# Another written order for the same operations of attention and a two-layer network

## The chip, the cores and the metric

The kernel runs on one core of a Trainium2 chip. A core has five engines, each with its own list of instructions: PE (TensorE, matrix multiplication), ACT (ScalarE), DVE (VectorE), POOL (GpSimd) and SP (SyncE, which here only issues transfers). DMA transfers are issued by SP, ACT or POOL. The metric is the time of one execution on the device in microseconds (us); lower is better. The numbers of runs are medians.

## The reference

Eight batches of eight heads have 576 tokens of 64 dimensions each, and every head has 16 extra "beacon" keys and values that stand ahead of its own and that every token sees. Causal attention over them gives 4608 rows of 512 features; these go through a layer of 2048 units with a squared ReLU and back to 512.

```python
k_all = np.concatenate([beacon_k, k], axis=2)
v_all = np.concatenate([beacon_v, v], axis=2)
scores = scale * np.matmul(q, k_all.transpose(0, 1, 3, 2))
scores = np.where(causal, -1000000000.0, scores)
...
a = np.exp(scores)
a /= a.sum(-1, keepdims=True) + 1e-09
attn = np.matmul(a, v_all)
...
h = x @ w_in
r = np.maximum(h, 0.0)
g = r * r
return (g @ w_out).astype(np.float32)
```

Inputs and the output are fp32; the kernel multiplies in bf16.

## The kernel before

The work is cut into 1553 operations. Each has a name, an engine or a choice of engines, the operations that it needs, and the buffers that it takes from small pools: two pairs of PSUM banks for scores (`strip`), four single banks (`ps`), six fp32 staging buffers (`stg`). The string `SEQUENCE` at the head of the file (lines 16 to 149) writes the names in one order. `Order.run` walks it word by word, takes the buffers, and emits the operation's instructions; a letter behind `@` says on which engine (A is ACT, D is DVE, P is POOL). Nothing is rearranged afterwards, so this one string sets the order on each engine, the order in each queue of transfers, and which buffer each operation gets. An engine takes its instructions strictly in that order: one that waits holds up all behind it.

The names that matter below:

- `fldq`, `fldk`: the first loads of batch 0's q (issued by ACT into osb1) and k (issued by SP into osb0), for the first 240 tokens: head pair 0 alone, pair 1 alone, and pairs 2 and 3 together. `fcq`, `fck` cast them to bf16 (L351 is a copy or cast on ACT, L353 one on DVE or POOL).
- `sld`: loads that cast on the way (L473), issued by POOL, for the rest of batch 0's q and k and all of batch 1's. `two` joins two heads of such a load side by side. `ld` (L397, L398) loads 128 tokens into a staging buffer, and `cast` turns them to bf16: so come the v of batches 0 and 1 (POOL's queue) and everything of the later batches (SP's queue). `bkl` loads the beacon keys (L443).
- `ident`, `tri`: the identity matrix and the causal mask, made by POOL. `fill`: sixteen dummy matrix multiplications of 128x512 that only keep PE busy (L485).
- `tp`: transposes on PE of q and k of batches 0 and 1 (L511), copied out of PSUM by ACT or DVE (`eq`, `ek`); `tpb` does the beacon keys (L453). Later batches are transposed by DMAs on SP's queue (`tr`, L432).
- `qk`: scores (L649); `exp`: their exponentials on ACT (L671 in batch 0, L747 later); `mask` (L770, DVE); `av`: weighted sums of v (L792); `norm`: division by the sums (L809, L811, DVE). `xtp`, `xte` (L860) and, from batch 3 on, transposing DMAs `xt` (L843) bring the result to xT.
- `s1`: the first layer of a chunk of 512 tokens (L1094, in the last two chunks L971), then `relu` and `sq` on ACT or DVE; `s2`: the second layer (L1144, L1203), its evacuations `ev` (L351, L353, L1226), and the stores `st` (L1132; in the last chunk L1257). From the third chunk on the second layer, and in the last two also the first, replaces one of eight block products by sums (`wsum`, `asum`, `xsum`, `sum`). `win` and `wout` (L884, L892) load the weights in quarters by POOL's queue. The first load of batch 2 waits for the quarter `wout3`.

Batches 0 and 1 go through PE transposes and start the pipeline; then the scores of a batch, the first layer of a chunk and the second layer of the chunk before are woven into one stream on PE.

Of the kernel before, what the change touches and what calls it, by code (L numbers as in the profile page):

```python
# [16 lines left out]
fldk1 fldk0 bkl0 fldk2 sld0q1.0 sld0k1.0 ident sld0k1.2 sld0q1.2 tri ld0v0 ld0v1 ld0v2 ld0v4 fldq0 fldq2 fldq1 fcq2@A  # L17
bkc0 fck2 fill14 fill1 fill3 fill0 fill4 fill9 fill7 tp0.0.2q tp0.0.2k tpb0 fcq1 tp0.0.1q fck3 fcq3@D fcq0 ek0.0.2@D
ekb0 fck1 bkl1 ld0v3 two0.1.3k@P sld1q0.0 sld1k0.0 two0.1.3q@P cast0v0@P win0 cast0v2 cast0v4 sld1k0.2 cast0v3 ld1v4
win1 sld1q0.2 two1.0.0k@P win3 ld1v2 ld1v3 two1.0.2k@P cast1v4 win2 ld1v1 ld1v0 wout0 wout1 two1.0.2q@P wout3 wout2  # L20
two1.0.3k@P cast1v3 cast1v1 cast1v2 cast1v0 two1.0.3q@P fck0 tpg0.0.2k eq0.0.2@A tpg0.0.2q tp0.0.1k tp0.0.3k ek0.0.1@A
ek0.0.3@A tpg0.0.3k tpg0.0.1k qk2.0.0 tp0.0.0q exp2.0.0 eq0.0.0@A two0.1.1q@D eq0.0.1@D tp0.0.3q fill10 two0.1.0q@D
eq0.0.3@D tpg0.0.1q tpg0.0.0q two0.1.0k@D two0.1.1k@D tpg0.0.3q qk1.0.0 exp1.0.0 qk3.0.0 fill13 tp0.0.0k tp0.1.1k
ek0.0.0@A tpg0.0.0k bkc1 ek0.1.1@D tpg0.1.1k exp3.0.0 fill15 tp0.1.1q qk0.0.0 fill5 tp0.1.0q fill6 eq0.1.1@A tpg0.1.1q
eq0.1.0@D mask2.0.0 exp0.0.0 qk1.1.0 tp0.1.0k qk1.1.1 exp1.1.0 ek0.1.0@D mask3.0.0 two0.1.2q@D mask0.0.0 two0.1.2k@D
tpg0.1.0q qk0.1.0 exp1.1.1 exp0.1.0 mask1.1.1 mask1.0.0 cast0v1@D fill11 qk1.1.2 fill2 tp0.1.2k tp0.1.3k tp0.1.3q
qk0.1.1 exp1.1.2 ek0.1.2@A mask1.1.0 eq0.1.3@A ek0.1.3@D tpg0.1.2k tpg0.1.3k tpg0.1.3q tpg0.1.0k mask0.1.1 qk0.1.2
exp0.1.1 exp0.1.2 av1.0.0 fill8 av3.0.0 qk3.1.0 tp0.1.2q norm1.0.0 norm3.0.0 eq0.1.2@A mask0.1.0 tpg0.1.2q av0.0.0
av2.0.0 norm0.0.0 two1.0.0q@D exp3.1.0 norm2.0.0 qk3.1.1 xtp0.0.3 av1.1.0 xte0.0.3@A exp3.1.1 norm1.1.0 fill12 qk2.1.0
exp2.1.0 two1.0.1k@D two1.0.1q@D mask2.1.1 mask3.1.1 qk3.1.2 tpb1 xtp0.0.0 mask3.1.0 ekb1 av0.1.0 xte0.0.0@A norm0.1.0  # L30
qk2.1.2 tp1.0.0k tp1.0.0q tp1.0.1q exp3.1.2 exp2.1.2 ek1.0.0 tpg1.0.0k qk2.1.1 eq1.0.0@D eq1.0.1@A tpg1.0.1q tpg1.0.0q
exp2.1.1 av3.1.0 xtp0.0.2 xtp0.0.1 xte0.0.1@A norm3.1.0 tp1.0.1k xte0.0.2@A qk4.2 xtp0.1.3 mask2.1.0 ek1.0.1 tpg1.0.1k
xte0.1.3@D exp4.2.1.0.0 exp4.2.0.0.0 av2.1.0 s1.0.1.0 s1.0.2.0 norm2.1.0 xtp0.1.0 xtp0.1.1 qk4.4 relu0.1.0@A mask4.0.0
xte0.1.0@A xte0.1.1@D relu0.2.0@A exp4.4.0.0.0 s1.0.4.0 xtp0.1.2 s1.0.5.0 xte0.1.2@D relu0.5.0@A s1.0.0.0 s1.0.1.1
tp1.0.2k relu0.0.0@D relu0.4.0@D exp4.4.1.0.0 relu0.1.1@A s1.0.0.1 ek1.0.2 relu0.0.1@A s1.0.7.0 s1.0.3.0 relu0.7.0@A
relu0.3.0@D s1.0.5.1 relu0.5.1@A tp1.0.2q eq1.0.2@A s1.0.3.1 s1.0.6.0 tpg1.0.2q tpg1.0.2k qk5.7 relu0.3.1@D
relu0.6.0@A sq0.2.0@A exp5.7.-1.0.0 s1.0.4.1 relu0.4.1@A exp5.7.-1.1.0 sq0.1.0@A s1.0.6.1 s1.0.15.1 relu0.6.1@D
mask4.0.2 sq0.0.1@D s1.0.13.0 s1.0.12.1 relu0.15.1@A mask4.0.1 relu0.13.0@A relu0.12.1@A exp5.7.1.0.0 sq0.3.0@A
s1.0.7.1 s1.0.13.1 s1.0.14.1 relu0.7.1@D relu0.13.1@A s1.0.9.1 relu0.9.1@A s1.0.9.0 s1.0.8.1 relu0.14.1@A relu0.9.0@D
sq0.0.0@A relu0.8.1@D s1.0.11.1 s1.0.11.0 s1.0.10.1 relu0.11.0@D sq0.2.1@A relu0.11.1@D av4.0.0 s1.0.2.1 av4.0.1  # L40
sq0.3.1@A relu0.10.1@D exp5.7.0.0.0 relu0.2.1@A norm4.0.0 sq0.5.1@D norm4.0.1 s1.0.14.0 relu0.14.0@A s1.0.8.0
relu0.8.0@A sq0.1.1@A sq0.7.1@D sq0.4.1@A s1.0.10.0 s1.0.15.0 s1.0.12.0 relu0.12.0@A sq0.6.0@A relu0.10.0@D sq0.5.0@A
s2.0.2.0 relu0.15.0@D tp1.0.3k sq0.6.1@A mask5.0.1 s2.0.2.1 tp1.0.3q s2.0.0.0 ek1.0.3 sq0.7.0@D mask5.0.0 tpg1.0.3k
eq1.0.3@A tpg1.0.3q qk7.13 exp7.13.-1.1.0 exp7.13.-1.0.0 sq0.4.0@D exp7.13.0.0.0 exp7.13.1.0.0 s2.0.0.1 wsum1
mask5.0.2 av5.0.0 s2.0.3.0 norm5.0.0 s2.0.0.2 s2.0.2.2 s2.0.0.3 s2.0.3.1 ev0.0@A qk6.10 exp6.10.-1.1.0 exp6.10.-1.0.0
zero2 ld2k0 ld2q0 ld2q1 ld2q2 ld2q3 ld2k1 cast2q1 cast2q0 cast2k0 cast2q3 cast2q2 ld2q4 ld2k2 cast2q4 cast2k1 ld2k3
ld2k4 cast2k2 cast2k3 tr2q cast2k4 tr2k ld2v0 ld2v1 ld2v2 ld2v3 ld2v4 ld3k0 zero3 cast2v2 cast2v0 s2.0.3.2 av5.0.1
s2.0.2.3 s2.0.3.3 s2.0.1.0 mask7.0.1 wsum2 exp6.10.1.0.0 exp6.10.1.0.1 exp6.10.0.0.0 ev0.2@A mask6.0.0 mask6.0.2
mask7.0.2 mask7.0.0 mask6.0.1 norm5.0.1 ev0.3@A av6.0.0 av7.0.0 av6.0.1 s2.0.1.1 norm7.0.0 norm6.0.0 av7.0.1 xtp1.0.1
norm6.0.1 xte1.0.1@D norm7.0.1 s2.0.1.2 xtp1.0.2 xtp1.0.0 xtp1.0.3 s2.0.1.3 xte1.0.3@D xte1.0.2@A xte1.0.0@A ev0.1@A  # L50
warm s1.1.14.0 s1.1.13.0 relu1.13.0@D s1.1.6.0 s1.1.1.0 s1.1.9.0 relu1.14.0@A relu1.6.0@D s1.1.12.0 s1.1.4.0
relu1.1.0@A relu1.9.0@A relu1.12.0@D st0 cast2v4 cast2v3 cast2v1 ld3q0 cast3q0 ld3q1 ld3q2 cast3q1 ld3q3 ld3k1 ld3q4
ld3k2 cast3q3 cast3q2 cast3k1 ld3k3 ld3k4 cast3q4 st1 tr3q cast3k0 cast3k3 cast3k2 cast3k4 tr3k ld3v0 ld3v1 ld3v2
cast3v2 cast3v0 ld3v3 cast3v3 cast3v1 ld3v4 ld4k0 ld4q0 ld4q1 ld4q2 cast4k0 cast3v4 qk8.4 exp8.4.1.0.0 exp8.4.0.0.0
s1.1.0.0 s1.1.3.0 s1.1.15.0 relu1.0.0@D relu1.15.0@D sq1.0.0@D relu1.4.0@A qk8.2 exp8.2.0.0.0 s1.1.7.0 s1.1.2.0
s1.1.5.0 relu1.7.0@A exp8.2.1.0.0 relu1.2.0@D relu1.3.0@A sq1.1.0@A mask8.0.1 relu1.5.0@D mask8.0.2 sq1.2.0@D
# [1304 lines left out]
```

## Time and profile before

| | |
|---|---|
| median of 3 runs | 330.6 us (330.38 to 331.23) |
| profiled execution, its span from the first instruction to the last | 329.0 us |
| median less that span | 1.6 us |
| PE busy in the span | 314.3 us (96%) |
| DVE, ACT, POOL busy | 235.9, 218.2, 100.5 us |
| granted TensorE clock, mean | 1.000 |

For the profiled execution the profile gives its span; the row below that is the difference to the runs' median. In the views, PEld is the weight load of TensorE, which runs beside PE, and SPq, ACTq and POOLq are the engines' queues in the act of issuing a transfer. "<-" behind a row names what the engine waited for.

### The profile page before, as it was taken

The numbers are of one execution on the slowest core, as the hardware profiler recorded it, in microseconds if no ns is written. First come the engines' busy times: TensorE is split into PE (matmuls) and PEld (weight loads), VectorE is DVE, ScalarE is ACT, GpSimd is POOL, SyncE is SP. The second block draws the span as 40 slices with busy tenths as digits, with TensorE's granted clock in tenths as the row PEclk, the third lists the DMA queues.
The fourth block names the chain that finished last, engine by engine and source line by source line (L and its number), as shares of the span: only waits on it lengthen the run. The fifth ranks groups of instructions, "written<-read, shape, count | busy, mean of one in ns | idle before, by whom it ended". The sixth has DMA issues, their size and how long they took to land.

```text
span 329.0 us, 8399 instructions
## 1 busy us (share of the span) xinstructions
PE 314.3 (96%) x3407; PEld 225.1 (68%) x3428; DVE 235.9 (72%) x503; ACT 218.2 (66%) x324; POOL 100.5 (31%) x157
## 2 busy tenths in 40 slices
PE   4789999999999999999999999999999999999995
PEld 1357885554556448778886566666878788888884
DVE  1799467445745699758973878657788699598982
ACT  2599996546953996678577567679852493895710
POOL 8997704414504704025032502531200320000000
PEclk9999999999999999999999999999999999999999
DMA  8999998999999995299999997998941500011033
GB/s 165 215 213 224 220 187 193 200 196 241 234 199 194 235 210 108 65 185 216 182 191 195 214 202 192 215 171 172 180 111 66 136 2 0 2 61 68 3 143 114
DMA packets 145601, 51.97 MB, mean 158 GB/s; under 512 B 132506, under 2 KB 140570, under 8 KB 145562
## 3 DMA queue, kind: packets, MB, share of 16 engines
q1 hardware_dynamic: 135901, 42.32, 62.7%
q0 software_dynamic: 8512, 8.49, 15.1%
q10 hardware_dynamic: 1149, 0.62, 0.7%
q8 instruction: 27, 0.44, 0.6%
q14 instruction: 12, 0.10, 0.1%
HBM read 37.22 MB, written 9.44 MB: 142 GB/s over the span
## 4 chain that ended last, share of the span: by engine, by line
PE 76%; DMA 9%; SPq 6%; DVE 3%; POOL 2%; issue 2%; ACT 1%; POOLq 0%; DVEq 0%; ACTq 0%
PE ps L1094 24%; PE ps L1203 18%; PE ps L1144 8%; PE ps L792 8%; PE strip L649 4%; PE strip L971 4%; DMA stg<-in_v_dram 3%; PE ps L971 3%; PE strip L1203 2%; DMA osb<-in_k_dram 2%; SPq L843 2%; SPq L432 2%; PE ps L649 1%; SPq L398 1%; DMA stg<-in_q_dram 1%
## 5 line engine op out<-in xcount | busy, mean ns | idle before, releaser
L1094 PE MATMUL ps<-xT,w_in 128*128 128x512 bf16 (+6 forms) x627 | 103.7, 314 | 1.0 <-DMA xT<-xn 0.3
L747 ACT ACTIVATE pt<-strip 128x1024 bf16<-128x1024 f32 (+3 forms) x77 | 71.0, 958 | 15.4 <-PE strip L649 14.3
L1094 PEld LDWEIGHTS <-w_in 128*128 128x128 bf16 x640 | 56.9, 98 | 35.4 <-issue 1.9
L1109 ACT ACTIVATE g<-ps 128x512 bf16<-128x512 f32 (+2 forms) x74 | 38.9, 545 | 27.1 <-PE ps L1094 26.0
L353 POOL CAST qk_area<-stg 128x512 bf16<-128x512 f32 (+2 forms) x60 | 39.6, 685 | 54.6 <-DMA stg<-in_q_dram 49.5
L353 POOL CAST vb<-stg 128x512 bf16<-128x512 f32 (+1 forms) x39 | 25.8, 682 | 82.7 <-DMA stg<-in_v_dram 69.3
L1111 DVE TENSOR_SCALAR g<-ps 128x512 bf16<-128x512 f32 (+2 forms) x54 | 33.2, 623 | 23.5 <-PE ps L1094 23.0
L1203 PEld LDWEIGHTS <-g 128*128 128x128 bf16 x448 | 42.5, 98 | 7.3 <-issue 1.8
L770 DVE TENSOR_TENSOR pt<-pt,tri 128x512 bf16<-128x512 bf16 (+1 forms) x93 | 37.6, 427 | 6.7 <-ACT pt L747 6.4
L792 PEld LDWEIGHTS <-pt 128*128 128x128 bf16 x930 | 35.5, 99 | 7.1 <-issue 0.9
L792 PE MATMUL ps<-vb,pt 128*128 128x65 bf16 x930 | 38.1, 194 | 0.8 <-POOL vb L353 0.6
L1203 PE MATMUL ps<-w_out,g 128*128 128x256 bf16 x304 | 38.8, 273 | 0.0
L1203 PEld LDWEIGHTS <-sum_area 128*128 128x128 bf16 x336 | 31.8, 98 | 5.5 <-issue 1.0
L811 DVE TENSOR_TENSOR xn<-ps,rcp 128x320 bf16<-128x320 f32 (+2 forms) x64 | 31.5, 491 | 2.5 <-DVE rcp L809 0.4
L1119 ACT ACTIVATE g<-g 128x1024 bf16<-128x1024 bf16 (+2 forms) x35 | 31.5, 928 | 0.5
L1144 PE MATMUL ps<-w_out,g 128*128 128x512 bf16 x120 | 29.9, 379 | 0.4
L747 ACT ACTIVATE pt<-ps 128x512 bf16<-128x512 f32 x42 | 23.6, 600 | 8.5 <-PE ps L649 8.5
L649 PE MATMUL strip<-qT,kT 64*128 64x208 bf16 (+15 forms) x406 | 27.4, 255 | 0.7 <-ACT pt L671 0.4
L649 PEld LDWEIGHTS <-kT 64*128 64x128 bf16 x520 | 17.3, 94 | 15.0 <-issue 10.3
L1203 PE MATMUL ps<-w_sum,sum_area 128*128 128x256 bf16 x208 | 26.7, 273 | 0.0
L809 DVE RECIPROCAL rcp<-ps 128x5 f32<-128x5 f32 (+2 forms) x64 | 12.1, 189 | 16.2 <-PE ps L792 15.2
L351 ACT COPY osb<-ps 128x512 f32<-128x512 f32 x22 | 12.9, 588 | 15.5 <-PE ps L1203 11.6
(99 smaller groups left out, 375.1 us busy)
## 6 DMA issues: line engine op xcount, KB each, us to landing
out_dram<-osb SPq DMA_DIRECT2D x16, 512.0 KB, 4.1
stg<-in_q_dram SPq DMA_DIRECT2D x24, 256.0 KB, 4.8
stg<-in_k_dram SPq DMA_DIRECT2D x18, 256.0 KB, 4.4
stg<-in_v_dram SPq DMA_DIRECT2D x18, 256.0 KB, 4.6
w_in<-in_moe_w_in_dram POOLq DMA_DIRECT2D x4, 512.0 KB, 9.1
w_out<-in_moe_w_out_dram POOLq DMA_DIRECT2D x4, 512.0 KB, 12.3
stg<-in_v_dram POOLq DMA_DIRECT2D x6, 256.0 KB, 8.5
stg<-in_k_dram SPq DMA_DIRECT2D x6, 224.0 KB, 4.2
```

The lines of the kernel that those rows point to most:

```text
L353: eng[e].tensor_copy(dst, src)
L649: nc.tensor.matmul(out, kT[b % 2][hp, pr, 128 * c:128 * c + 128], rhs, start=True, stop=True)
L747: nc.scalar.activation(out, in_, AF.Exp, bias=0.0, scale=scale)
L770: nc.vector.tensor_tensor(out=d, in0=d, in1=tri[0:rows, m0:m0 + m, 0:w][:, None].to_broadcast([rows, 2, m, w]), op=ALU.min)
L792: nc.tensor.matmul(a[0:w, at + (t - tl[0]) * (D + 1):at + (t - tl[0] + 1) * (D + 1)], P[0:rr, hj, o:o + w], vb[b % 2][0:rr, c, 2 * pr + hj ...
L811: nc.vector.tensor_tensor(out=xn[b % 2].rearrange("p t (h d) -> p h t d", d=D)[:, h0:h0 + nh, tl[0]:tl[0] + nt], in0=a[:, :, :, 0:D], in1= ...
L1094: nc.tensor.matmul(h[:, lo - spans[0][0]:hi - spans[0][0]], w_in_sb[:, mc, ft * 128:(ft + 1) * 128], xT[:, mc, lo % RING:lo % RING + hi - lo],
L1109: nc.scalar.activation(dst, h, AF.Relu, bias=0.0, scale=1.0)
L1111: nc.vector.tensor_scalar(out=dst, in0=h, scalar1=0.0, scalar2=None, op0=ALU.max)
L1119: nc.scalar.activation(d, d, AF.Square, bias=0.0, scale=1.0)
L1144: nc.tensor.matmul(o, G[:, fc, ts * 128:(ts + 1) * 128], w_out_sb[:, fc, :], start=(fc == 0), stop=(fc == NFT - 1))
L1203: nc.tensor.matmul(o, lhs[:, f, t * 128:(t + 1) * 128], rhs[:, f], start=fresh and f == 0, stop=f == HF - 1, skip_group_check=True)
```

## The change

Only the string `SEQUENCE` differs. It holds the same 1553 names in another order, with other letters for 152 of them: 77 go from DVE to ACT, 69 from ACT to DVE, three from POOL to DVE and three from DVE to POOL. The new string is a line longer, so that every line of the code behind it has a number higher by one. The head and the end of the difference:

```diff
 SEQUENCE = """
-fldk1 fldk0 bkl0 fldk2 sld0q1.0 sld0k1.0 ident sld0k1.2 sld0q1.2 tri ld0v0 ld0v1 ld0v2 ld0v4 fldq0 fldq2 fldq1 fcq2@A
...
-ev8.c22.1 s2.8.3.1 s2.8.4.1 ev8.c12.0 ev8.c21.0@D st8.0.1.0 st8.0.0.256 st8.0.0.0 st8.1.0.0 ev8.c12.1 ev8.c21.1@A
-st8.0.1.256 st8.1.1.0
...
+ev8.c21.0@D st8.1.0.0 s2.8.3.0 ev8.c12.0 st8.0.0.256 ev8.u2.1@A s2.8.7.1 ev8.u3.1@A s2.8.5.1 s2.8.4.1 ev8.c21.1@A
+ev8.c22.1 s2.8.3.1 st8.0.0.0 ev8.c12.1 st8.0.1.256 st8.1.1.0
```

On ACT at the start of the program, before (osb1 is where q of batch 0 is loaded, qT and kT hold the transposed q and k, strip the scores; a load of 120x2x128 is one head pair, one of 120x4x128 is two):

```order
L554 DMA osb1_83<-in_q_dram 120x2x128
L554 DMA osb1_83<-in_q_dram 120x4x128
L554 DMA osb1_83<-in_q_dram 120x2x128
L351 ACT_TABLE_LOAD
L351 CAST qk_area_64<-osb1_83 120x2x2x64 x3
L351 COPY qT0_68<-ps3_94 128x240
L351 COPY kT0_70<-ps1_92 128x240
L351 COPY kT0_70<-ps0_91 128x240
L671 ACTIVATE pt_72<-strip0_89 128x2x368
```

The same place after:

```order
L555 DMA osb1_83<-in_q_dram 120x4x128
L555 DMA osb1_83<-in_q_dram 120x2x128 x2
L352 ACT_TABLE_LOAD
L352 CAST qk_area_64<-osb1_83 120x2x2x64 x2
L352 COPY qT0_68<-ps2_93 128x240
L352 CAST qk_area_64<-osb1_83 120x2x2x64
L352 COPY kT0_70<-ps0_91 128x240
L352 COPY qT0_68<-ps3_94 128x240
L352 COPY qT0_68<-ps1_92 128x240
L672 ACTIVATE pt_72<-strip0_89 128x2x368
```

The load of two pairs of q is now the first; the two single ones follow, pair 1 and then pair 0. The cast of q's pair 2 has gone to DVE, and that of pair 3 has come from there. On SP's queue, in the same way, the load of k for pairs 2 and 3 moved from the fourth place to the second, and pair 0's from the second to the fourth.

On POOL at the start, before (stg are the staging buffers of v, qk_area takes the casting loads of q and k):

```order
L473 DMA qk_area_64<-in_q_dram 112x4x192
L473 DMA qk_area_64<-in_k_dram 112x4x192
masks.py:197 MEMSET ident_77 128x128
masks.py:199 ISA
masks.py:199 AFFINE_SELECT ident_77<-ident_77 128x128
L473 DMA qk_area_64<-in_k_dram 112x4x192
L473 DMA qk_area_64<-in_q_dram 112x4x192
L336 MEMSET tri_88 128x512
L338 AFFINE_SELECT tri_88<-tri_88 128x128 x4
L397 DMA stg_63<-in_beacon_v_dram 16x8x64
L398 DMA stg_63<-in_v_dram 112x8x64
L398 DMA stg_63<-in_v_dram 128x8x64 x2
```

The same place after:

```order
L399 DMA stg_63<-in_v_dram 128x8x64
masks.py:197 MEMSET ident_77 128x128
masks.py:199 ISA
masks.py:199 AFFINE_SELECT ident_77<-ident_77 128x128
L474 DMA qk_area_64<-in_q_dram 112x4x192
L474 DMA qk_area_64<-in_k_dram 112x4x192
L337 MEMSET tri_88 128x512
L339 AFFINE_SELECT tri_88<-tri_88 128x128 x4
L474 DMA qk_area_64<-in_q_dram 112x4x192
L474 DMA qk_area_64<-in_k_dram 112x4x192
L474 DMA qk_area_64<-in_q_dram 96x4x384
L398 DMA stg_63<-in_beacon_v_dram 16x8x64
```

One load of v (`ld0v3`) goes ahead of the identity, all four casting loads behind it, and the first casting load of batch 1 (96x4x384) ahead of the other four loads of v.

On ACT at the end of the program, before (g holds the squared first layer of the last chunk, osb the output on its way to the store):

```order
L1048 ACTIVATE g_80<-g_80 128x1024 x2
L351 COPY osb_82<-strip_89 128x256
L351 COPY osb_83<-ps_92 128x2x256
L351 COPY osb_83<-strip_90 128x256
L1257 DMA out_dram<-osb_82 128x256
```

The same place after:

```order
L1049 ACTIVATE g_80<-g_80 128x1024 x5
L352 COPY osb_83<-ps_93 128x2x256
L352 COPY osb_82<-strip_90 128x256
L352 COPY osb_82<-strip_89 128x256
L352 COPY osb_83<-strip_90 128x256
L352 COPY osb_82<-strip_89 128x256
L352 COPY osb_83<-strip_89 128x256 x2
L1258 DMA out_dram<-osb_82 128x256
```

ACT takes more of the last evacuations. On PE the last product of all, `s2.8.3.1` now and `s2.8.4.1` before, is therefore followed by an addition on DVE (`ev8.c12.1`) and the half-width store on ACT's queue, where an ACT copy (`ev8.c21.1`) and the full-width store on SP's queue followed before.

In between, names move by a few places nearly everywhere. The order of w_out's quarters on POOL's queue is 1, 3, 0, 2 in place of 0, 1, 3, 2, with casts of batch 1's v between them; batch 2's DMA transposes, the scores of batches 2 and 3, and the loads of batches 4 and 5 stand earlier among PE's work, the DMA transposes `xt4.4`, `xt5.4` and `xt7.3` later.

More of the change, by code (lines that the diff above doesn't have):

```diff
@@ L22 @@
[L22 to L56, printed above, removed]
```

227 lines of the change are left out of this document (131 added, 96 removed).

## The prediction

> **What bounds the kernel now.** I read the page's busy shares and its 40 slices first, to see which engine is the limit and where it is not:
>
> ```profile
> span 329.0 us, 8399 instructions
> PE 314.3 (96%) x3407; PEld 225.1 (68%) x3428; DVE 235.9 (72%) x503; ACT 218.2 (66%) x324; POOL 100.5 (31%) x157
> PE   4789999999999999999999999999999999999995
> ```
>
> PE works for 314.3 us of 329.0. The multiplications are the same in both kernels, so at most 329.0 - 314.3 = 14.7 us of idle PE can be won, and the PE row puts it at both ends: its first slices read 4, 7 and 8, its last 5. The view by windows gives it exactly (after the window's length come the busy us of PE, weight loads, DVE, ACT and POOL, each with a count, then granted clock, DMA share and GB/s):
>
> ```profile
> 0.00:8.00 8.00, 3.37 (x9) 1.15 (x9) 0.87 (x6) 2.11 (x4) 6.70 (x17) 1.00 0.88 165
> 8.00:16.00 8.00, 5.70 (x43) 2.71 (x43) 6.31 (x15) 4.21 (x10) 7.88 (x12) 1.00 1.20 215
> 12.00:32.00 20.00, 18.16 (x284) 11.76 (x281) 18.26 (x50) 18.10 (x30) 17.17 (x25) 1.00 1.21 215
> 32.00:320.00 288.00, 285.96 (x3060) 206.95 (x3079) 211.00 (x435) 196.72 (x288) 72.65 (x112) 1.00 0.77 154
> 320.00:329.00 9.00, 5.10 (x47) 4.31 (x45) 2.86 (x7) 0.37 (x1) 0.00 (x0) 1.00 0.29 104
> ```
>
> From 32 to 320 us PE idles for 288.00 - 285.96 = 2.04 us in all. A new order can win no more than that in the nine tenths of the span where the stream of scores, first layer and second layer runs; it can lose any amount there. The rest, 8.8 us before 32 and 3.9 us after 320, is where the written order can pay. Two things show in the first 32 us: until 12 us PE waits, and from 12 to 32 DVE (18.26 of 20) and ACT (18.10) are as full as PE (18.16), so three engines share the limit.
>
> What PE waits for at the start is in the table of PE's waits (total us, times, longest) and, in order of time, in the chain that ended last (start, us, what):
>
> ```profile
> PE ps L485 <- POOL ident masks.py:199: 3.5, 1, 3.5
> PE ps L511 <- DVE qk_area L353: 3.4, 2, 2.6
> PE ps L792 <- POOL vb L353: 0.6, 2, 0.4
> PE ps L1094 <- DMA xT<-xn: 0.3, 1, 0.3
> ```
>
> ```profile
> 2.23 6.87 DMA osb<-in_k_dram
> 9.12 1.06 DVE qk_area L353 x3
> 11.77 0.46 PE strip L649 x4
> 12.23 0.52 PE ps L511 x4
> 12.75 0.43 PE ps L485
> ```
>
> The chain is plain: the load of k for head pairs 2 and 3, the last of the k loads on SP's queue, issued at 2.23, lands at 9.10; DVE casts it; PE transposes it, and the first scores (L649) follow at 11.7. PE also waited 3.5 us for the identity matrix, and 2.6 us in one piece for that cast.
>
> **The change part by part.** *The first loads.* The new order puts k of pairs 2 and 3 second on SP's queue, and q of pairs 2 and 3 first on ACT's, with q of pair 0 third. POOL issues one load (256 KB of v) before the identity where it issued two casting ones (168 KB each), so the bytes ahead of the first loads do not grow.
>
> ```profile
> 0.81 1.56 ACTq L554 DMA_DIRECT2D osb<-in_q_dram  x3
> 3.52 3.17 PE L485 MATMUL ps<-ident 128*128 128x512 bf16 x7 [3.52 <-POOL ident masks.py:199]
> 7.57 0.71 ACT L351 CAST qk_area<-osb 120x256 bf16<-120x256 f32 x2 [1.31 <-DMA osb<-in_q_dram]
> 5.86 0.40 ACT L351 CAST qk_area<-osb 120x256 bf16<-120x256 f32 x1 [2.17 <-DMA osb<-in_q_dram]
> 9.79 0.27 PE L453 MATMUL ps<-ident,bks 16*128 16x16 bf16 x4
> 11.70 0.53 PE L649 MATMUL strip<-qT,kT 64*128 64x240 bf16 x4
> osb<-in_q_dram ACTq DMA_DIRECT2D x1, 240.0 KB, 4.3
> ```
>
> The third q load released ACT at 7.57. I let q of pair 0, third in the new order with the same bytes before it, land at the same time; its cast of 0.40 ends at 7.97. Behind it PE has, before its first scores, six transposes (two for each of three loads: three times 0.26, from the chain's 0.52 for four), two dummy matmuls (0.43 each) and the beacon's transposes (0.27): 0.78 + 0.86 + 0.27 = 1.91, so the first scores start at 9.88 in place of 11.70. That is -1.8 us. The k load of pairs 2 and 3 must be landed and cast (0.35, a third of the chain's 1.06) when the first pair of those transposes is through, at 8.23. Issued second, at about 1.3, it lands at 5.6 if it takes the 4.3 of its like on ACT's queue, and at 8.2 if it takes the old 6.87, which would hold PE up for 0.3; being second in its queue it is nearer to the first, and I count nothing. The identity, behind one POOL issue and not two, comes some 0.7 earlier, but that only moves dummy matmuls, so I count nothing.
>
> *Does the start's gain reach the end of the stretch?* ACT's list up to its first 576-wide copy holds fifteen exponentials and eleven copies in both orders; one 240-wide copy of xT became a 240-wide and another a 336-wide one of q or k:
>
> ```profile
> 24.25 0.37 ACT L351 COPY xT<-ps 128x240 bf16<-128x240 bf16 x1
> 15.81 0.44 ACT L351 COPY qT<-ps 128x336 bf16<-128x336 bf16 x1
> ```
>
> That is +0.1 us at most on an engine with 20 - 18.10 = 1.9 us of idle time from 12 to 32. Since the whole list starts earlier, I carry the -1.8 through and set the +0.1 against the idle time: 0. The bounds are -1.9 (all that idle time goes as well) and +1.8 (all of the gain is lost).
>
> *The v loads of batch 0.* One of the five is now issued first, the others later on POOL's queue: v0 and v1, which the first weighted sums (L792) need, stand behind five casting loads and one v load, 256 + 4 x 168 + 288 = 1216 KB, where four casting loads (672 KB) stood ahead. POOL casts and issues in one list:
>
> ```profile
> 13.86 0.66 POOL L353 CAST vb<-stg 128x512 bf16<-128x512 f32 x1
> 20.57 0.36 PE L649 MATMUL strip<-qT,kT 64*128 64x208 bf16 x4
> 20.93 0.34 PE L792 MATMUL ps<-vb,pt 128*128 128x65 bf16 x6
> stg<-in_v_dram POOLq DMA_DIRECT2D x6, 256.0 KB, 8.5
> w_out<-in_moe_w_out_dram POOLq DMA_DIRECT2D x4, 512.0 KB, 12.3
> ```
>
> By the queue's service in the old trace, where such loads land some 1.3 us apart, v1 would land near 16.6 and be cast by 17.3, about when PE reaches those sums in the new order (the first scores' 1.8, and some two more because less stands ahead of them). I count 0. From the other side: an issue near 10.5 plus the median 8.5 gives 19.0, cast at 19.7, a PE wait of 2.4 us; with the 12.3 us of the slowest row on that queue it would be over 6. What hides this term is the work that stands ahead on PE; PE's order is fixed, so a late v1 stops the scores behind it too. [...]
>
> *The weights and later loads.* w_out's quarters come 1, 3, 0, 2, two of them behind casts of batch 1's v. Batch 2's first load waits for quarter 3, which moves from third to second, so the loads of batches 2 to 5 start earlier; scores of batches 2 and 3 have 3 to 5 us less work ahead of them on PE, and a few transposing DMAs into xT later. All of this lies under PE's full rows; the only direct row for such a wait is the 0.3 us above. I take 0, with bounds of -2.04 (all of PE's idle time from 32 to 320) and +3.1 (one transposing load late by its whole time, below).
>
> ```profile
> xT<-xn SPq DMA_TRANSPOSE x25, 3.1
> ```
>
> *The tail.* Before, the last product is followed by an ACT copy and a 256 KB store on SP's queue; now by a DVE addition and a 128 KB store on ACT's:
>
> ```profile
> 324.06 1.04 PE L1203 MATMUL strip<-w_sum,g 128*128 128x256 bf16 x8
> 324.26 0.42 DVE L1226 TENSOR_TENSOR osb<-ps,osb 128x256 f32<-128x256 f32 x1 [0.38 <-PE ps L1203]
> 325.18 0.37 ACT L351 COPY osb<-strip 128x256 f32<-128x256 f32 x1 [9.06 <-PE strip L1203]
> out_dram<-osb SPq DMA_DIRECT2D x2, 256.0 KB, 2.1
> out_dram<-osb ACTq DMA_DIRECT2D x1, 128.0 KB, 1.9
> ```
>
> 0.42 + 1.9 against 0.37 + 2.1 is -0.15 us. The 256 KB store now leaves one product earlier, and is done first.
>
> *Sum:* -1.8 + 0 + 0 + 0 - 0.15 = -1.95, a span of 327.05. The profiled execution gives a span of 329.0 against a median of 330.6, 1.6 us that lie around it in both, so 328.6 us.
>
> **The rivals.**
> [...]
> *The full stretch eats the gain (330.4).* DVE has 18.26 busy us in the 20 after 12; if its list, not the start, sets when the last exponential of batch 0 is released, PE only waits later, and the tail alone counts: 330.6 - 0.15. For it speaks the fullness of both engines; against it that three of four k pairs would be cast before the old 9.12, so DVE too begins earlier.
> *The full stretch gains as well (327.0).* If ACT's 1.9 us of idle time goes too, the sum is -3.6 to -3.85, 326.8 to 327.0. The trace has the same dummy matmul at two speeds:
>
> ```profile
> 14.94 0.63 PE L485 MATMUL ps<-ident 128*128 128x512 bf16 x1
> 16.16 0.39 PE L485 MATMUL ps<-ident 128*128 128x512 bf16 x1
> ```
>
> [...]
> *Slower: v1 late (332.6).* The place is the first L792 on PE. At 19.0 the wait of 2.4 us takes the gain and 0.45 more (331.0). It decides beyond +1.0, where v1 lands after about 19.6; at 20.6, two POOL issues or casts more, the wait is 4.0 and the time 330.6 - 1.95 + 4.0 = 332.6. For it speaks the median of 8.5 us to landing and the 544 KB more ahead of v1; against it that the queue, not the issue, sets the landing in the old trace.
> *Slower: a later wait (331.7).* One transposing load late by its 3.1 us takes the gain and 1.15 more. Against it: of 25 such loads one was waited for, for 0.3 us.
>
> **How the numbers follow.** A measurement of this kernel tells about 0.3% (1.0 us) from no change: the three runs before lie within 0.85 us. The forecast, 327.6 to 329.6, gets 0.43; the larger gain 0.15; the two rivals in which the gain is eaten 0.10 and 0.11, both within 1 us of before; v1 late 0.14, a later wait 0.07. Faster is 0.43 + 0.15 = 0.58, same 0.21, slower 0.21. The range takes in the larger gain at its low end (326.6) and the slower case up to v1 at 20.6 (332.6); what is left out is the farther part of both slow cases, about 0.1, and less than 0.05 below.
>
> **What would show it.** Right: the first scores near 9.9, the first L792 without a wait of over 1 us for vb, the last scores of batch 0 about 1.8 us earlier than the old row
>
> ```profile
> 28.37 0.35 PE L649 MATMUL strip<-qT,kT 64*128 64x208 bf16 x6
> ```
>
> the idle time of PE from 32 on still near 2 us, and a chain that ends on a DVE addition. Wrong on the loads: PE waits for a q or k cast past 8.3. Wrong on v: a new row among PE's waits, from L792 for vb, of 2 us or more, or scores waiting for ACT right after. Wrong on the stream: waits of L1094 for xT, or of the scores for a batch's loads, of more than a microsecond.

## The result and the profile after

| | before | after |
|---|---|---|
| median of 15 runs each | 330.6 us (327.98 to 333.98) | 328.49 us (326.71 to 330.36) |
| ratio | | 0.9932, 95% interval 0.9906 to 0.9958 |
| span of the profiled execution | 329.0 us | 325.0 us |
| time of the profiled execution | | 326.74 us |

The change makes the kernel 0.7% faster. The two profiled executions differ by 4.0 us of span, the medians by 2.1: the one of after is among the shortest of its 15 runs, 1.75 us under their median. A reading of the two traces alone would make the change nearly twice as large.

The page of after, its first lines, PE's slices and the granted clock in tenths:

```profile
span 325.0 us, 8419 instructions
PE 314.7 (97%) x3428; PEld 225.4 (69%) x3428; DVE 234.9 (72%) x495; ACT 224.7 (69%) x332; POOL 105.2 (32%) x157
PE   5889999999999999999999999999999999999995
PEclk9799999999999999999999999999999999999999
```

PE's work is the same, and its first slices are fuller (5, 8, 8 where 4, 7, 8 stood). New is the 7 in the second slice of the clock. The view by windows (columns as in the prediction):

```profile
0.00:8.00 8.00, 4.14 (x15) 1.60 (x16) 2.36 (x11) 2.70 (x5) 6.72 (x17) 1.00 0.78 164
8.00:16.00 8.00, 7.15 (x64) 3.64 (x65) 5.44 (x15) 6.86 (x13) 8.00 (x12) 0.79 1.34 213
12.00:32.00 20.00, 18.03 (x296) 12.65 (x296) 17.46 (x49) 17.71 (x29) 18.17 (x25) 0.95 1.24 218
32.00:316.00 284.00, 283.76 (x3051) 204.85 (x3046) 210.32 (x426) 200.18 (x290) 76.28 (x112) 1.00 0.77 157
```

From 8 to 16 us PE and ACT work 7.15 and 6.86 us where they had 5.70 and 4.21; from 12 to 32 nothing is won, PE works as long as before. From 32 to 316 PE idles for 0.24 us instead of 2.04, but most of that difference lies in the records and not in the kernels: the old page has only 3407 of 3428 matmuls. The second trace of the new kernel (below) has 3406 and idles for 1.96 us there; that of the old order with only the loads of q moved has all 3428 and idles for 0.50.

PE's waits after, and the places that the prediction named, from the timeline:

```profile
PE ps L486 <- POOL ident masks.py:199: 3.0, 1, 3.0
PE ps L512 <- DVE g L354: 1.4, 2, 0.9
PE strip L650 <- ACT pt L672: 0.6, 2, 0.4
PE ps L793 <- DVE vb L354: 0.2, 1, 0.2
```

```profile
7.52 0.40 ACT L352 CAST qk_area<-osb 120x256 bf16<-120x256 f32 x1
7.62 0.38 PE L486 MATMUL ps<-ident 128*128 128x512 bf16 x1 [0.85 <-ACT qT L352]
9.13 0.87 PE L650 MATMUL strip<-qT,kT 64*128 64x240 bf16 x8
10.92 0.63 PE L486 MATMUL ps<-ident 128*128 128x512 bf16 x1
14.78 0.39 PE L486 MATMUL ps<-ident 128*128 128x512 bf16 x1
16.47 0.78 POOL L354 CAST vb<-stg 128x512 bf16<-128x512 f32 x1
17.59 0.34 PE L793 MATMUL ps<-vb,pt 128*128 128x65 bf16 x6 [0.16 <-DVE vb L354]
26.20 0.35 PE L650 MATMUL strip<-qT,kT 64*128 64x208 bf16 x6
```

The wait for k's cast (3.4 us before) is gone. The first scores start at 9.13 instead of 11.70, the first weighted sums at 17.59 instead of 20.93, the last scores of batch 0 at 26.20 instead of 28.37. Against the old row of 11.70 that is -2.57 us, and -2.17 at the last scores: a little is given back in the full stretch. The dummy multiplications show PE fast at 7.62 (0.38 us), slow again at 10.92 (0.63) and fast at 14.78, whereas the old trace was slow to 14.94 and fast from 16.16 on. When PE becomes fast differs from execution to execution of the same start, as the table near the end shows, so these differences belong to this pair of traces.

The chain at the end, and the tail:

```profile
320.41 0.89 PE ps L1204 x8
321.29 0.02 issue
321.32 0.42 DVE osb L1227
```

From the start of the last evacuation to the end it takes 3.7 us (325.0 - 321.32), before 3.8 (329.0 - 325.18).

### The profile page after: what moved, and what is told of

Read it like the earlier page. It is cut to its first block, busy times and chain, and to the rows that moved or that the text cites. A ratio compares the mean times of both kernels' runs of the same rounds, so it can differ in the third digit from the quotient of the medians.

```text
span 325.0 us, 8419 instructions
## 1 busy us (share of the span) xinstructions
PE 314.7 (97%) x3428; PEld 225.4 (69%) x3428; DVE 234.9 (72%) x495; ACT 224.7 (69%) x332; POOL 105.2 (32%) x157
## 4 chain that ended last, share of the span: by engine, by line
PE 93%; DVE 2%; DMA 2%; issue 1%; ACT 0%; POOL 0%; DVEq 0%; POOLq 0%
PE ps L1095 30%; PE ps L1204 25%; PE ps L793 9%; PE ps L1145 9%; PE strip L650 6%; PE strip L972 4%; PE ps L972 3%; PE strip L1204 2%; PE ps L650 2%; DMA qk_area<-in_q_dram 2%; PE ps L512 1%; PE ps L861 1%; PE ps L486 0%; DVE xn L812 0%; DVE qT L354 0%
## 5 line engine op out<-in xcount | busy, mean ns | idle before, releaser
L748 ACT ACTIVATE pt<-strip 128x1024 bf16<-128x1024 f32 (+3 forms) x77 | 70.2, 952 | 10.1 <-PE strip L650 9.9
L354 POOL CAST qk_area<-stg 128x512 bf16<-128x512 f32 (+2 forms) x60 | 41.2, 712 | 48.7 <-DMA stg<-in_k_dram 24.9
L354 POOL CAST vb<-stg 128x512 bf16<-128x512 f32 (+1 forms) x39 | 27.7, 722 | 76.6 <-DMA stg<-in_v_dram 76.6
L1112 DVE TENSOR_SCALAR g<-ps 128x512 bf16<-128x512 f32 (+2 forms) x54 | 32.8, 614 | 20.0 <-PE ps L1095 17.3
L771 DVE TENSOR_TENSOR pt<-pt,tri 128x512 bf16<-128x512 bf16 (+1 forms) x93 | 35.8, 410 | 8.3 <-ACT pt L748 7.9
L793 PEld LDWEIGHTS <-pt 128*128 128x128 bf16 x930 | 34.9, 99 | 6.2 <-issue 1.2
L1204 PE MATMUL ps<-w_out,g 128*128 128x256 bf16 x304 | 38.0, 273 | 0.0
L793 PE MATMUL ps<-vb,pt 128*128 128x65 bf16 x930 | 37.6, 194 | 0.2 <-DVE vb L354 0.2
L1120 ACT ACTIVATE g<-g 128x1024 bf16<-128x1024 bf16 (+2 forms) x31 | 28.4, 944 | 5.6 <-DVE g L1112 5.3
L1145 PE MATMUL ps<-w_out,g 128*128 128x512 bf16 x128 | 31.1, 379 | 0.0
L352 ACT COPY osb<-ps 128x512 f32<-128x512 f32 x24 | 14.1, 590 | 20.9 <-PE ps L1204 16.2
L650 PE MATMUL strip<-qT,kT 64*128 64x128 bf16 (+15 forms) x406 | 27.5, 256 | 0.6 <-ACT pt L672 0.6
```

The costliest lines, as they stand in the source:

```text
L354: eng[e].tensor_copy(dst, src)
L650: nc.tensor.matmul(out, kT[b % 2][hp, pr, 128 * c:128 * c + 128], rhs, start=True, stop=True)
L748: nc.scalar.activation(out, in_, AF.Exp, bias=0.0, scale=scale)
L771: nc.vector.tensor_tensor(out=d, in0=d, in1=tri[0:rows, m0:m0 + m, 0:w][:, None].to_broadcast([rows, 2, m, w]), op=ALU.min)
L793: nc.tensor.matmul(a[0:w, at + (t - tl[0]) * (D + 1):at + (t - tl[0] + 1) * (D + 1)], P[0:rr, hj, o:o + w], vb[b % 2][0:rr, c, 2 * pr + hj ...
L1112: nc.vector.tensor_scalar(out=dst, in0=h, scalar1=0.0, scalar2=None, op0=ALU.max)
```

## The experiments

Theory: the gain is made before the first scores, by the order of the first loads, and the full stretch behind passes it on; the rest of the new order gives nothing. Rivals: the later stream makes the gain; the loads are not the cause; the stretch is limited by DVE; PE's clock decides. Ratios are to the old kernel run beside each, with 95% intervals. The old kernel's median was 330.64 us beside the new start, the new rest, the first loads and the new kernel again, 330.53 beside k alone, q alone, v behind the casting loads and batch 0 without masks, and 330.1 beside the other four. Medians of kernels from different groups can differ by that half microsecond alone; the ratios take it out. All are of 12 runs, but for the repeat of the new kernel (7), the kernel without masks (6) and the one with more dummy multiplications (6).

### The new start alone

The new order up to the scores of pair 6, then the old one; the words at the joint:

```diff
 ev0.0@A qk6.10 exp6.10.-1.0.0 exp6.10.-1.1.0
-cast3q0 s2.0.3.1 exp6.10.1.0.0
+wsum1 s2.0.3.1 s2.0.3.2 av5.0.1 s2.0.2.3 s2.0.3.3
```

> The new order up to the scores of pair 6 (some 55 us into the program), then the old order for all the rest, its tail too. Theory A (the gain arises at the start, about 2.5 us of the profiled pair's 4.0, and some 1.3 us more arise in the stream after 160 us): a trace that leads the old one by about 2.5 us at 60 us and by no more than that at the end, and a median 1.3 to 2.5 us under the old kernel's. Rival B (the stream evens out any early lead, and the gain is made after 160 us): the lead of 2.5 us at 60 us is gone by 320 us, and the median is within 0.5 us of the old one. Rival C (the start alone carries the whole median gain of 2.1 us): the median equals the new kernel's.

Measured: 0.9941 (0.9912 to 0.9969), 328.14 us. The start alone carries the gain within the uncertainty of the measurement. Its trace is of its longest execution and is not read here.

### The new rest alone

The old order up to the same place, then the new:

```diff
 ld3k0 zero3 cast2v2 cast2v0
-s2.0.3.2 av5.0.1 s2.0.2.3
+warm cast2v1 cast2v3 cast2v4 ld3q0 ld3q1 mask7.0.1
```

> The old order up to the same place, then the new one. Theory A: no lead at 60 us, 1 to 1.5 us at 320 us (the waits of L792 for a cast of v near 173 and 208 us and of L1094 for xT near 242 us are gone), 0.15 from the tail, so a median about 1.2 to 1.6 us under the old kernel's. Rival B: nearly the whole gain, 2 us or more. Rival C: within 0.5 us of the old kernel.

Measured: 0.9995 (0.9965 to 1.0024), 330.36 us. Theory A's 1.2 to 1.6 us for the stream lie just outside the interval (1.16 us at its lower end), and rival B's 2 us well outside. The waits of the old trace for v near 173 and 208 us belong to that execution: the traces of the next kernels below, with the same order there (the first loads, k alone, q alone), don't have them. The wait for xT near 242 us they do have, with 0.2 to 0.3 us. The earlier loads of the new order don't show in the median, and the tail's 0.1 to 0.2 us is too small for it. Rival C stands: the start alone.

### The first loads alone

```diff
-fldk1 fldk0 bkl0 fldk2 sld0q1.0
+fldk1 fldk2 bkl0 fldk0 sld0q1.0
...
-ld0v4 fldq0 fldq2 fldq1 fcq2@A
+ld0v4 fldq2 fldq1 fldq0 fcq2@A
```

> The old kernel with only the first loads on SP's and ACT's queues in the new order (k of pairs 2 and 3 second, q of pairs 2 and 3 first, q of pair 0 last); all engines keep the old order. Theory A1 (the load of k for pairs 2 and 3 was the wait, and the order of the loads alone gives the start's gain): k of pairs 2 and 3 lands near 6.6 instead of 9.1, the first scores start at 9.2 to 9.7 instead of 11.7, lead near 2.2 us at 30 us, median 1.5 to 2.2 us under the old kernel's. Rival A2 (the order on PE, DVE and ACT matters as much, since the old lists cast and transpose what now lands late before the first scores, and POOL delays the rest): first scores after 10.5, lead at 30 us below 1 us, median within 0.8 us of the old one.

Measured: 0.995 (0.9923 to 0.9976), 329.27 us, some 1.65 us by the ratio and 1.4 by the medians. In its timeline:

```profile
7.97 0.67 DVE L353 CAST qk_area<-osb 120x256 bf16<-120x256 f32 x3
8.30 0.28 PE L511 MATMUL ps<-ident,qk_area 120*128 120x120 bf16 x2 [1.41 <-DVE qk_area L353]
9.70 0.52 PE L649 MATMUL strip<-qT,kT 64*128 64x240 bf16 x4
```

Second in its queue, the load of k for pairs 2 and 3 takes 5.3 us from issue to landing in the trace of after, where it took 6.9 before. Here DVE, which first casts the beacon keys that it had waited for until 7.37, begins to cast k at 7.97 instead of 9.12, and the first scores start at 9.70, as A1 said. Another order for six loads on two queues, with every engine's other work left as it was, gives most of the gain: 1.65 of about 2. Whether the engines' new order adds to it can't be told: the intervals of this kernel and of the new start overlap.

### The new kernel again

```diff
 SEQUENCE = """
 fldq2 fcq2@D ld0v3 ident fill6 fill5
```

> The new kernel again, unchanged, for a second trace and second set of times beside the others. Expected 326.7 to 330.4, median 328.5; a trace in which the lead at 60 us lies between 1.5 and 2.7 us.

Measured: 0.9922 (0.9891 to 0.9953), 327.71 us (325.99 to 329.13). With the first 15 runs, 22 of the same program have a median of 328.27 us. The runs list the mean granted clock of each: in 6 it is 0.997 or more, with a median time of 327.22; in 8 under 0.992, with 329.0. In 83 runs of the old kernel the same two groups have 330.27 (45 runs) and 330.33 (26). So a lower clock goes with 1.8 us in the new kernel, and with none to speak of in the old. With only the first loads moved it is the other way round: the five runs at 0.997 or more have a median of 329.97, the seven below of 328.39. The table near the end shows why this column is hard to read.

Its trace is ahead of that of after: the first scores start at 8.89 and the last of batch 0 at 25.09, 3.28 us before the old row, with a clock of 1.00 throughout.

### Only k, only q

```diff
-fldk1 fldk0 bkl0 fldk2 sld0q1.0
+fldk1 fldk2 bkl0 fldk0 sld0q1.0
```

> The old kernel with only SP's first loads in the new order (k of pairs 2 and 3 second, of pair 0 last). If the load of k for pairs 2 and 3 was the whole wait: it lands near 6.6 instead of 9.1, first scores 9.7 to 10.6, and the gain of the change of both queues (0.5%, 1.65 us) comes back whole, 1.3 to 1.9 us. If q's order carries half of it: 0.6 to 1.0 us.

```diff
-ld0v4 fldq0 fldq2 fldq1 fcq2@A
+ld0v4 fldq2 fldq1 fldq0 fcq2@A
```

> The old kernel with only ACT's first loads in the new order (q of pairs 2 and 3 first, of pair 0 last). If k was the whole wait: first scores stay at 11.7 (the wait for k's cast at 9.1 remains), and the median within 0.4 us of the old one. If q's order carries half: 0.6 to 1.0 us faster.

Measured: k alone 0.9956 (0.9926 to 0.9987), 329.29 us; q alone 0.9967 (0.9944 to 0.9989), 329.52 us. Both are faster, and together they give 0.995: the two don't add up, and the intervals don't rank them. k alone brings the first scores to 8.89 in its trace, q alone to 11.26. That k was the main wait is what the traces say, but single traces differ by as much as is at stake: the same old start gives 11.70 in the old kernel's trace and 10.64 in that of the new rest, where PE was fast from 6.57 us on. That q alone should give over 1 us, where its expectation with k as the whole wait was 0.4 at most, is not explained by its 0.44 us there, and stays open.

### v behind the casting loads

```diff
-fldq2 fcq2@D ld0v3 ident fill6
+fldq2 fcq2@D ident fill6
...
-tp0.0.1q sld0k1.2 fill13
+tp0.0.1q sld0k1.2 ld0v3 fill13
```

> The new kernel with its first load on POOL's queue (256 KB of v) moved behind the four small casting loads. Theory (the bytes ahead of the first loads do not grow, since two casting loads of 168 KB stood there before): q of pair 0, which landed at 7.50, comes at 7.2 to 7.8, first scores within 0.4 us of 9.13, median within 0.5 us of the new kernel's. Rival (v first holds up the first loads, by 256 KB at 165 GB/s): q of pair 0 near 5.9 to 6.5, first scores 1 to 1.6 us earlier, median 1 us or more faster.

Measured: 0.9963 (0.9934 to 0.9992), 329.49 us. Slower than the new kernel by about 1 us, which neither side had said. Rows of its timeline:

```profile
1.43 2.74 PE L486 MATMUL ps<-ident 128*128 128x512 bf16 x6 [1.43 <-POOL ident masks.py:199]
5.70 0.78 PE L512 MATMUL ps<-ident,qk_area 120*128 120x120 bf16 x6 [1.53 <-ACT qk_area L352]
7.79 0.41 ACT L352 CAST qk_area<-osb 120x256 bf16<-120x256 f32 x1
9.66 0.63 PE L486 MATMUL ps<-ident 128*128 128x512 bf16 x1
10.23 0.88 PE L650 MATMUL strip<-qT,kT 64*128 64x240 bf16 x8
```

The last cast of q starts at 7.79 against 7.52, so v at the head of the queue doesn't hold the first loads up; the rival of the expectation is refuted. The price of 1 to 1.6 us that it has, my estimate from 256 KB at the 165 GB/s of the old trace's first window, does not show: with the casting loads first in POOL's queue that cast comes 0.27 us later and not earlier. What differs in this trace is PE. With nothing ahead of the identity the dummy multiplications run from 1.43 to 4.17, PE then waits 1.53 us, and a dummy one still takes 0.63 us at 9.66.

That this wait is the price is not shown. The trace is of the fastest of the 12 executions, 327.88 us with a clock of 1.000, below the new kernel's median; ten others have a clock of 0.990 or less and a median of 329.5. And the new kernel's own start, with the identity at 3.01, left PE just as slow in other traces (0.64 us at 9.41 without masks, 0.63 at 9.01 with more dummy multiplications).

### That kernel with three more dummy multiplications

```diff
-fcq3@A fcq1 tp0.0.3q
+fcq3@A fcq1 fill16 fill17 fill18 tp0.0.3q
...
-    NFILL = 16
+    NFILL = 19
```

> The kernel with v behind the four casting loads, which was 0.3% slower than the new one, with three more dummy multiplications behind the first six, so that PE is busy from 1.4 us to the first transposes at 5.7 without the 1.5 us of waiting. If the loss came from that wait (its dummy multiplications at 8.7 and 9.7 us still took 0.63 us): fast multiplications (0.38 us) by 8 us, first scores at 9.2 to 9.6 instead of 10.23, median 0.7 to 1.2 us under that kernel's. If it came from the loads themselves: first scores after 9.9, median within 0.4 us of that kernel's.

Measured: 0.9941 (0.9911 to 0.9971), 328.62 us, 0.9 us better than that kernel by the medians, 0.7 by the ratios, with overlapping intervals. So the gain is at the low end of what was expected of the wait, and not clear of none. The trace shows PE fast early and slow again later:

```profile
7.13 0.38 PE L486 MATMUL ps<-ident 128*128 128x512 bf16 x1 [0.66 <-ACT qT L352]
21.64 0.61 PE L486 MATMUL ps<-ident 128*128 128x512 bf16 x1
```

```profile
8.00:16.00 8.00, 6.75 (x74) 3.40 (x73) 6.56 (x18) 7.65 (x15) 7.48 (x11) 1.00 1.25 225
16.00:24.00 8.00, 6.33 (x67) 3.62 (x64) 4.81 (x17) 5.67 (x9) 8.00 (x12) 0.57 1.27 217
```

PE is fast from 7.13, and the first scores come at 8.68, the earliest of all traces and earlier than expected. Then, from 16 to 24 us, the granted clock is 0.57, a dummy multiplication takes 0.61 again, and ACT has 5.67 busy us of 8: the last scores of batch 0 start at 27.24, later than in the trace of after.

### No dummy multiplications

```diff
-            if e != "-":
+            if e != "-" and not (name.startswith("fill")):
                 op.insts = op.emit(e)
```

> The new kernel without its sixteen dummy multiplications (left out; they compute nothing that is used). If the speed of PE's matmuls in the first 16 us matters (a dummy one takes 0.61 to 0.63 us slow and 0.38 to 0.39 fast, and the new kernel's traces are fast from 7.6 us on): the same multiplications stay slow to 14 us or more, first scores later than 9.6 us, lead at 30 us smaller by 1 us or more, median 1 us or more over the new kernel's. If the order of the loads and of ACT's list alone sets the start: lead and median within 0.5 us of the new kernel's.

Measured: 0.9972 (0.9955 to 0.999), 329.27 us, about 1 us over the new kernel. The first scores start at 9.02, and not after 9.6 as expected of a slow PE, so the start itself doesn't need them; but PE stays slow deep into the full stretch:

```profile
26.03 0.57 PE L650 MATMUL strip<-qT,kT 64*128 64x208 bf16 x4
28.62 0.35 PE L650 MATMUL strip<-qT,kT 64*128 64x208 bf16 x6
```

The granted clock of all its 12 runs is 0.998 or more, although its matmuls are slow up to 26 us. So that column does not count the slow time before PE's first rise; it counts a fall after it. The stretch from the first to the last scores of batch 0 takes 19.60 us here, against 16.20 in the second trace of the new kernel, which points to a price of PE's speed of its own.

### Batch 0 without its masks

```diff
-            if e != "-":
+            if e != "-" and not (name[:6] in ("mask0.", "mask1.", "mask2.", "mask3.")):
                 op.insts = op.emit(e)
```

> The new kernel without the causal masks of batch 0 (twelve multiplications on DVE, 4 to 5 us of its work between 12 and 26 us, left out, so batch 0's output is not the reference's). Theory (in the full stretch DVE's list is what PE waits for, so part of the early lead of 4 us is given back there): the lead at 28 us grows from 2.5 to about 4, median 1 to 2 us under the new kernel's. Rival (ACT's exponentials are the limit there, or the loads): the lead at 28 us grows by less than 0.5 us, median within 0.5 us of the new kernel's.

Measured: 0.9894 (0.9851 to 0.9938), 326.71 us in 6 runs.

```profile
12.00:32.00 20.00, 18.81 (x300) 12.90 (x299) 13.02 (x39) 18.02 (x31) 17.22 (x24) 1.00 1.23 222
```

DVE loses 4.4 of its 17.46 us, and ACT works 18.02 (17.71 in after). The last scores of batch 0 start at 26.11, against 26.20, and its first scores were 0.84 us later than those of after: at most some 0.9 us of the full stretch depended on DVE's masks. Beside the second trace of the new kernel, whose clock didn't fall either, nothing did: 16.14 us from the first to the last scores here, 16.20 there. So the lead is that of the rival, while the median, lower by 1.6 us, is that of the theory; its interval overlaps the new kernel's, and six runs don't settle it.

### Three exponentials twice

```diff
-                    nc.scalar.activation(prob(p)[:, :, off:off + width], st[:, :, 0:width],
-                                         AF.Exp, bias=0.0, scale=scale)
+                    for _ in range(2 if (p, n, i) in ((0, 0, 0), (0, 1, 0), (1, 1, 2)) else 1):
+                        nc.scalar.activation(prob(p)[:, :, off:off + width], st[:, :, 0:width],
+                                             AF.Exp, bias=0.0, scale=scale)
```

> The new kernel with three of batch 0's exponentials between 14 and 20 us issued twice (0.78, 0.87 and 0.95 us, 2.6 us more work on ACT; the same result). If ACT's list is the limit of the full stretch (ACT is busy 4.00 of 4 us from 16 to 20 in the new kernel's trace): the last scores of batch 0 come 2 to 2.6 us later, median 1.8 to 2.6 us over the new kernel's. If ACT has room there, and DVE or PE limits: later by less than 1 us.

Measured: 1.0037 (1.0017 to 1.0057), 331.23 us: 2.96 us over the 328.27 of the new kernel (3.6 by the ratios), for 2.6 us of added work on ACT.

```profile
16.16 4.05 ACT L673 ACTIVATE pt<-strip 128x736 bf16<-128x736 f32 x5
PE strip L650 <- ACT pt L673: 1.4, 2, 0.9
24.00:32.00 8.00, 7.80 (x112) 5.04 (x112) 5.55 (x19) 5.49 (x8) 5.98 (x8) 1.00 1.25 228
```

ACT runs without a gap there, and PE waits for its exponentials for 1.4 us, where it waited 0.6 in after. What is put on ACT's list in this stretch comes out at the end, and more than it. The rest is PE's: in this trace, of the slowest of the 12 executions, PE is slow until past 28 us (0.57 us for four scores at 28.43), ACT in turn waits for scores (5.49 busy us of 8 from 24 to 32), and the last scores of batch 0 come at 32.06, 5.9 us after those of after and not the 2 to 2.6 expected. Ten of the 12 executions have a clock of 0.984 or less. So from 12 to 20 us, where ACT is busy 3.85 and then 4.00 of 4 us in after too, ACT's list is what the stretch waits for, and an earlier first exponential (9.69 against 12.27) is what the kernel keeps. That ACT alone limits the rest of the stretch is not shown, since in this trace the added work goes with a slower PE.

### More dummy multiplications where PE waits

```diff
-    NFILL = 16
+    NFILL = 24
...
-tp0.1.1q fck3
+fill16 fill17 tp0.1.1q fck3
...
-tp0.1.2k eq0.1.2@A
+fill20 fill21 fill22 tp0.1.2k eq0.1.2@A
```

> The new kernel with eight more dummy multiplications on PE (24 in all), at the places where PE waits between 10 and 22 us: two ahead of the second part's first transposes, one each ahead of two score groups, three ahead of the last transposes of pair 2, one ahead of the first xT transposes. If short idle times let the clock fall again in the middle of the stretch (runs of the new kernel with a mean clock of 0.997 or more have a median of 327.2, those under 0.992 of 329.0): nearly all runs at 0.995 or more, median 326.8 to 327.6, 0.5 to 1.3 us under the new kernel's. If the clock falls for another reason: clocks as before, median within 0.3 us of the new kernel's, or 0.3 to 0.8 us over it where the added ones get in the way.

Measured: 0.9896 (0.9867 to 0.9925), 326.84 us (325.46 to 327.4) in 6 runs, the clock at 0.997 or more in five of them and 0.992 in the sixth.

```profile
16.00:24.00 8.00, 7.40 (x107) 4.45 (x104) 6.87 (x23) 7.58 (x12) 8.00 (x12) 1.00 1.26 216
```

This version beats the old kernel by 1.04% and has the lowest median of the versions that compute the whole output, 1.4 us under the new kernel's (1.1 by the ratios). Its interval and that of the new kernel's first runs (0.9906 to 0.9958) overlap a little, so that it is better than the new kernel is likely, not settled. Nor is it shown that the added multiplications hold the clock up: in this trace PE becomes fast only at 12.40 us, so there was no early rise to fall back from, and of the other five executions only the mean clock is on record.

## Why the prediction was right, and where its steps were not

The time (328.6 forecast, 328.49 measured), the sign and the place were right; some of the terms were not.

The traces also hold the clock's own entries, which the views only show as means: from when PE was granted the full clock (1.0), and from when to when half of it (0.5). Times are in us, and "stretch" is the time from the first to the last scores of batch 0.

| trace | PE fast from | slow again | first scores | last scores | stretch |
|---|---|---|---|---|---|
| before | 15.56 | | 11.70 | 28.37 | 16.67 |
| q alone | 14.87 | | 11.26 | 27.96 | 16.70 |
| new rest (the old start) | 6.57 | 9.98 to 16.81 | 10.64 | 28.65 | 18.01 |
| k alone | 6.70 | 10.12 to 13.53, 27.18 to 30.59 | 8.89 | 27.17 | 18.28 |
| first loads | 7.49 | 10.90 to 14.31 | 9.70 | 27.08 | 17.38 |
| after | 7.21 | 10.62 to 14.04 | 9.13 | 26.20 | 17.07 |
| after, second trace | 7.68 | | 8.89 | 25.09 | 16.20 |
| without masks | 15.89 | | 9.97 | 26.11 | 16.14 |
| more dummy multiplications | 12.40 | | 9.57 | 26.37 | 16.80 |
| v moved back | 12.55 | | 10.23 | 26.93 | 16.70 |
| v moved back, three more | 6.76 | 17.00 to 23.83 | 8.68 | 27.24 | 18.56 |
| exponentials twice | 29.38 | | 9.61 | 32.06 | 22.45 |
| no dummy multiplications | 27.94 | | 9.02 | 28.62 | 19.60 |

A mean clock of 1.00 thus says only that the clock did not fall: it reads so in traces with PE fast from 7.68 us and from 27.94.

- **What bounds the kernel, right in the place.** The gain lies at the start. The new start alone gives 0.9941, the new rest 0.9995. The 2.04 us of idle time from 32 us on, which the prediction took as the bound for the later stream, was mostly missing records.
- **The first loads, right.** q of pair 0 was to be cast by 7.97; its cast ran from 7.52 to 7.92. k of pairs 2 and 3 was no longer waited for. From the end of q's cast to the first scores the prediction had 1.91 us; it took 1.2 in the three traces in which PE was fast by then (after, its second trace, v moved back with three more), and 1.9 to 2.0 in the four in which it was slow (without masks, more dummy multiplications, exponentials twice, v moved back). The -2.57 of the profiled pair sets a slow old trace beside a fast new one. Like with like, the first scores come 1.7 to 2.1 us earlier with PE slow (9.97, 9.61 and 9.57 against 11.70) and 1.5 to 1.8 with PE fast (9.13 and 8.89 against 10.64), which is near the forecast's -1.8 in both. The kernel with only the loads moved gave 1.65 us by its ratio.
- **The identity, open.** It came 0.5 us sooner, as about foreseen (0.7), and I counted nothing because it only moves dummy multiplications. The kernel with v moved back had it at 1.43 instead of 3.01 and was some 1 us slower by its median; no trace shows why.
- **The full stretch, right where the clock doesn't fall.** I carried the start through unchanged. The stretch takes 16.1 to 16.8 us in the six traces, of both orders, in which PE is fast by 16 us and stays so, and 17.1 to 18.6 in the five in which it falls back. The trace of after is one of these and gave 0.4 us back; its second trace gave back nothing. The +0.1 of copies on ACT I set against ACT's idle time; from 16 to 20 us, where ACT is busy 4.00 of 4 us in after, there is none.
- **v, right.** v1 near 16.6 and cast by 17.3 was the forecast; POOL's cast of it ran from 16.47 to 17.25, and L793 waited 0.16 us, for v0's cast on DVE. The slower rival didn't come about.
- **The later stream, 0 as forecast.** The profiled pair differs by 2.17 us at the last scores of batch 0 and by 4.0 at the end, but the new rest alone measures 0.9995.
- **The tail, -0.15:** the traces show -0.1; no run could resolve it in the time.
- **The larger gain, half right, with its price unforeseen.** I gave it 0.15, with the two speeds of the dummy multiplication beside it. PE leaves its slow rows earlier in both traces of after (7.21 and 7.68, against 15.56), but the old start did so too in one trace (6.57), and the new start left them only at 12.40 and 15.89 in two others, so the new order is not shown to be the reason. In the 6 of 22 runs whose clock stayed up the median is 327.22, near its 327.0; the runs with a low clock have 329.0. What I had no term for is that a PE that is fast early can fall back, as it did at 10.62 us in after. With such a spread from one execution to the next, that the forecast lies within 0.1 us of the median is in part luck.

What sets PE's speed is not shown. Every fall in the table lasts 3.41 us or twice that. PE, busy from 3.01, was fast from 7.21 in after and from 7.68 in its second trace. But in the trace without masks, with the same start and PE counted busy 4.00 of 4 us from 8 to 12, a dummy multiplication still took 0.63 us at 14.13, so an early and full PE was not enough for an early rise there. In after PE fell at 10.62, busy 7.15 of the 8 us from 8 to 16 and, from 3.01 on, without a wait of over 0.9 us. That short waits bring a fall about was only a theory of the run with more dummy multiplications; no run shows it.

Open: what sets when PE becomes fast and in which execution the clock falls, how much of the median gain goes through that, why q's order alone gave over 1 us, and whether the engines' new order at the start is worth anything beside the loads.

## What to carry to other kernels

Where one late load at the start holds the first chain up, look first at its place in its queue: another order for six loads gave most of what a new order of 1553 operations gave (1.65 of about 2 us). The lead at the start was here worth about what the engine that is full behind it started earlier (ACT's first exponential at 9.69 instead of 12.27, the last scores of batch 0 at 26.20 instead of 28.37). Busy shares alone didn't tell that engine from the others (DVE 18.26, ACT 18.10 and PE 18.16 of 20 us before); adding to or taking from one list told more (2.6 us more on ACT's list cost 2.96 by the medians, 4.4 us less on DVE's gave at most some 0.9 of the stretch), and the trace must show what else the edit changed, PE's speed above all. In a stretch in which PE waits often and briefly, a few dummy multiplications in the gaps may be worth more than the time they take (326.84 us in six runs against 328.27, not settled). A pair of single traces is a poor measure of a 1% change (4.0 us between the spans here, 2.1 between the medians); where it has to serve, compare traces in which PE became fast at like times.

## What the hardware showed that I had not expected

- The mean granted clock reads 1.00 in windows in which the same dummy multiplication takes 0.63 instead of 0.38 us, as long as PE has not been fast yet (slow to 26 us without dummy multiplications, clock 0.998 or more in all 12 runs).
- The same start makes PE fast at very different times: the new one from 7.21, 7.68, 12.40 or 15.89 us on, the old one from 6.57 or 15.56.
- PE can fall back to the slow speed after it has been fast, with waits of under a microsecond only: from 10.62 to 14.04 us in after, and from 17.00 to 23.83 in the kernel with v moved back and three more dummy multiplications, where the mean clock from 16 to 24 is 0.57. Every fall in the table above lasts 3.41 us or twice that.
- Starting the dummy multiplications 1.6 us earlier went with a slower kernel (0.9963 against 0.9932 and 0.9922), in which ten of twelve executions had a clock of 0.990 or less; no trace of one of these shows the reason.
